# State attention and a hard-swish FFN on one core: another order of the first 700 operations, shorter work in the first softmax, and a last tile copied in two halves

## The chip, the cores and the metric

The kernel runs on one core of a Trainium2 chip. The time is that of the device in microseconds (us), the median of the runs shown; less is better. TensorE is called PE (PEld: its weight loads), VectorE DVE, ScalarE ACT, GpSimd POOL and SyncE SP. SP issues most of the DMAs; ACT can issue them too, from its own queue.

## The reference

For 8 batches (B), 8 heads (H), 512 tokens (S), 32 states (Ns) and 64 columns (D):

```python
scores = scale * np.matmul(x, state.transpose(0, 1, 3, 2))
scores = scores - scores.max(-1, keepdims=True)
a = np.exp(scores)
a /= a.sum(-1, keepdims=True) + 1e-09
xread = np.matmul(a, state)
...
sread = np.matmul(a2, x)
```

`a2` is the same softmax the other way round, of the states over the tokens. The rows of `xread` and `sread` of one batch (512 + 32, heads side by side: 512 columns) go through `h = x @ w_in` (512 x 2048), `g = h * clip(h + 3, 0, 6) / 6` and `g @ w_out` (2048 x 512). All is in 32-bit floats.

## The kernel before, in words

**Tiling.** The work is cut into segments: one for each batch's 512 tokens, and a last one for all 256 state rows. A segment has 16 steps, one for each 128 rows of the hidden layer. A step's first product (`first`, line 959) gives 128 x 512 of h in one of two PSUM banks `ps_h`; ACT adds 3 and takes Relu (L1004), DVE does the minimum and the product (L1006), and g is split into a high and a low part (L306 on ACT, L307 on DVE), so that 32-bit accuracy comes from three matmuls of rounded parts each (L954). The second product (`second`, line 1013) adds g times 128 rows of w_out into four banks `acc0` to `acc3`, one for each 128 tokens (`j`). The weight that the first product uses isn't w_in but w' = state x w_in (`wprime`, line 547, matmuls at L512), so that xread is never made: h = a @ w'.

**The start.** Batch 0 has a way of its own. x and the state are loaded (L481, L438), PE turns them (L622, L593), ACT copies x to `xT` (L626). The turned state is copied four times into `apart` (part of the tile `sread_t`, L607), in two pairs, for either half `u` of the bank's partitions into either half `i` of the target's, and once whole as `stT` (L599): five reads of one bank. `tokens_by_rows` (line 669) makes the first softmax in four parts `q`: scores on PE (L687), maximum, subtraction (L699, L701), exponential on ACT (L704), sum, added constant, reciprocal and product on DVE (L706 to L711). PE turns the result back (L719) and ACT and DVE copy it to `a_first` (L721, L722). The first step (`plain`) takes its products in full 32-bit matmuls (L983, L1023). Weights arrive as 16-bit digits and are put together by ACT (L382) and DVE (L387, called a join here), then split into high and low halves (L414, L416). The big loads of w_in and w_out use tiles that later work needs: a load waits for its place.

**The order.** `Plan` (line 68) holds every operation with an engine (T: PE, V: DVE, S: ACT, Q: SP), a cost, a rank and what it depends on. `order` (line 102) sets them in a row: the first 700 or so are dictated by the list `OPENING`, numbers in the order in which the program adds operations; after it the planner takes the ready one with the lowest rank. Each engine then works through its own operations strictly in that order, so that one that waits holds up all behind it on its engine. `issue` (line 191) also puts matmuls on a constant tile (`wake`, L252; matmuls L1241) into the planned pauses of PE up to the first step. Waits themselves are put in by the framework, from what each instruction reads and writes; it also keeps two engines from using the same PSUM bank at once.

**The end.** The last segment has two tiles `j`. After the last step's second product DVE copies tile 0 out of its bank times 1/6 (L1050) and SP stores it; ACT copies tile 1 (L1047) and stores it from its own queue (L1070, shown with L1065).

Of the kernel before, what the change touches and what calls it, by code (L numbers as in the profile page):

```python
# [10 lines left out]
F32 = mybir.dt.float32  # L11
# [4 lines left out]
BF16 = mybir.dt.bfloat16  # L16
# [51 lines left out]
class Plan:  # L68
# [122 lines left out]
    def issue(self, tc, idle, until):  # L191

        with tc.manual_schedule(
            engines={ENGINE.PE, ENGINE.DVE, ENGINE.Activation, ENGINE.SP}
        ):
            last = 1.0
            for n in self.order():
                if self.ops[n][0] == "T":
                    if self.start[n] <= self.start[until]:
                        gap = self.start[n] - last  # L200
                        for _ in range(int((gap + 0.3) / 0.22) if last < self.WARM else int((gap - 0.25) / 0.13)):
                            idle()
                    last = self.start[n] + self.took[n]
                self.ops[n][3]()
# [3 lines left out]
def tile_state_attention_then_hardswish_ffn(  # L208
# [42 lines left out]
    wake = cpool.tile([P, 256], BF16, name="wake")  # L251
    nc.vector.memset(wake, 1.0)  # L252
# [179 lines left out]
    def load_state(b, rank, after=()):  # L432
        key = ("st_raw", b)

        def load():
            raw = get(key, lambda: att.tile([P, NG, D], F32, name="st_raw", bufs=1))
            for u in range(NG):
                nc.sync.dma_start(raw[:, u, :], st_v[b, :, :, u, :])  # L438
# [9 lines left out]
        if b < TURNED:  # L448
            plan.add("Q", 1.39, rank, load, (), [key], after, 400.0)
            return  # L450
# [137 lines left out]
    def take_in(b, rank, after=(), banks=None):  # L588
# [13 lines left out]
        for u in range(NG) if b < TURNED else ():  # L602
            for i in range(2):
                def put(u=u, i=i):
                    src = bank(st)[u * D : (u + 1) * D, :P].rearrange("p (q n) -> p q n", n=NS)
                    copy = nc.vector.tensor_copy if u == i else nc.scalar.copy
                    copy(apart[i * D : (i + 1) * D, :, u, i], src)  # L607
                (V if u == i else S_)(0.22, RANKS["apart"] if b == 0 else URGENT, put, [st], [("apart", b, u, i)])
# [60 lines left out]
    def tokens_by_rows(after, banks):  # L669
# [6 lines left out]
        whole = lambda: get(bt_key, lambda: outp.tile([P, J, DO], F32, name="ot")).rearrange(  # L676
            "p j e -> p (j e)")[:, : A * NQ * NS]
        wide = lambda t: t.unsqueeze(2).to_broadcast([P, A, NS])
        for q in range(NQ):
# [3 lines left out]
            def scores(q=q, ps=ps):  # L683
# [8 lines left out]
            bt = lambda q=q: whole().rearrange("p (a q n) -> p a q n", q=NQ, n=NS)[:, :, q]  # L692
            m1 = lambda m1_key=m1_key: get(
                m1_key, lambda: small.tile([P, S // NS], F32, name="m1"))[:, :A]
            total = lambda q=q: sums(0).rearrange("p g a -> p (g a)")[:, q * A : (q + 1) * A]
# [5 lines left out]
            shifted = V(0.35, r[1], lambda m1=m1, view=view, bt=bt: nc.vector.tensor_tensor(  # L701
                bt(), view(), wide(m1()), op=ALU.subtract), [m1_key, ps], [part_key])
            first_exps.append(shifted)
            S_(0.38, r[2], lambda bt=bt: nc.scalar.activation(bt(), bt(), AF.Exp, scale=SCALE),  # L704
               [], [part_key])
            V(0.34, r[3], lambda bt=bt, total=total: nc.vector.tensor_reduce(  # L706
                total(), bt(), axis=AX.X, op=ALU.add), [part_key], [sum_key])
            V(0.07, r[3], lambda total=total: nc.vector.tensor_scalar_add(total(), total(), 1e-9),
              [], [sum_key])
            V(0.11, r[3], lambda total=total: nc.vector.reciprocal(total(), total()), [], [sum_key])  # L710
            V(0.35, r[4], lambda bt=bt, total=total: nc.vector.tensor_tensor(  # L711
                bt(), bt(), wide(total()), op=ALU.mult), [sum_key], [part_key])
        for g in range(NG):
            back = (banks[g], ("B", 0, g))

            def turn(back=back, g=g):
                for j in range(J):
                    cols = slice((j * NG + g) * P, (j * NG + g + 1) * P)
                    nc.tensor.transpose(bank(back)[:, j * P : (j + 1) * P], whole()[:, cols], ident)  # L719
            T(0.47, RANKS["turn0"][0], turn, [(*bt_key, q) for q in range(NQ)], [back], after)  # L720
# [4 lines left out]
    def a_first(g):  # L725
        return w_in_of(2, "a", (P, NG, S))[:, g]
# [232 lines left out]
    def first(n):  # L959
        b, i, _, _ = steps[n]  # L960
        ps = ("ps_h", n)
        if b < B:
# [6 lines left out]
            reads += [(*wp_key(b, k), f0, u, h) for u in wide for h in ("hi", "lo")]  # L969
            if plain(b, i):  # L970
                reads = [("w_in2", "a", g) for g in wide]
                reads += [(*PLAIN_WP, f0, u) for u in wide]
# [7 lines left out]
        def run():  # L980
            if plain(b, i):
                for g in wide:
# [7 lines left out]
                [((wh[:, g, fs], wl[:, g, fs]), (ah[:, g, :], al[:, g, :])) for g in wide],  # L990
            )
        first_of[n] = T(1.95 if plain(b, i) else 1.37 if b < B else 1.45, n, run, reads, [ps], first_after.get(n, ()))
# [20 lines left out]
    def second(n):  # L1013
# [3 lines left out]
        for j in range(nt):  # L1017
# [13 lines left out]
            else:  # L1031
                T(0.685, n + LAG + 0.5, run,
# [6 lines left out]
        for j in range(nt):  # L1039
# [6 lines left out]
            elif (j % 2 == 0 or i < NF - 1) if b < B else j == nt - 1:  # L1046
# [13 lines left out]
        else:  # L1060

            ov = out.rearrange("(b s) e -> s b e", s=TOK)
            for j in range(nt):
                rows = slice(S + j * P // B, S + (j + 1) * P // B)
                store = lambda queue, j=j, rows=rows: queue.dma_start(ov[rows], ot()[:, j, :])  # L1065
                if j < nt - 1:
                    Q(n, 262.0, lambda store=store: store(nc.sync), [(*ot_key, j)])
                else:

                    S_(0.6, n, lambda store=store: store(nc.scalar), [(*ot_key, j)])  # L1070
# [146 lines left out]
    for n in range(len(steps)):  # L1217
# [7 lines left out]
        elif b < 1 and n % FPC == 0:  # L1225
            ends = wp_parts[b, c][1:] + [FPC]
            for f0, f1 in zip(wp_parts[b, c], ends):
# [3 lines left out]
                       ["acc2", "acc3"] if n == 0 and f1 < 3 else None,  # L1231
# [9 lines left out]
    plan.issue(tc, lambda: nc.tensor.matmul(awake[:, :256], wake[:, :P], wake, start=True, stop=True), first_of[0])  # L1241
# [30 lines left out]
```

## Time and profile before

| | |
|---|---|
| runs | 648.59, 648.62, 648.96 us |
| median | 648.62 us |
| the profiled execution | 649.16 us |
| its span, first to last instruction | 647.3 us |
| mean granted clock of TensorE | 0.998 |
| PE busy | 639.0 us (99%) |
| DVE busy | 393.3 us (61%) |
| ACT busy | 292.4 us (45%) |

The span is what the profile shows of the program; the profiled execution took 1.9 us more than it. A busy PE isn't PE at its peak, since matmuls are pipelined and overlap in the records. In rows in order of time the columns are: start in us, duration in us, engine, line, operation, out<-in, how many, and in brackets the engine's idle time before it with what ended it. In a table by stage, each engine has its busy time and its number of instructions.

### The profile page before, as it was taken

Reading aid. Unit: us, or ns where it says so; the run is one execution under the profiler, and the core shown is the slowest. Engines: PE = TensorE matmul, PEld = TensorE weight load, DVE = VectorE, ACT = ScalarE, POOL = GpSimd, SP = SyncE. Lnnn points to the kernel's source line nnn. Section 1 sums busy time; section 2 is a strip of 40 time slices with the busy share of each in tenths; the row PEclk is TensorE's granted clock in tenths of the full one; section 3 lists DMA queues with packets and bytes.
Section 4 is the critical chain, followed back from the end, with each engine's and each line's share of the span. In section 5 each row is a group of like instructions: output and inputs, shape, how many; then the busy total and the mean of one; then the engine's idle time right before and its main releaser. Section 6 shows DMA issues by size and latency. Waiting matters only on the chain.

```text
span 647.3 us, 9869 instructions
## 1 busy us (share of the span) xinstructions
PE 639.0 (99%) x3926; PEld 500.9 (77%) x3926; DVE 393.3 (61%) x685; ACT 292.4 (45%) x510; POOL 1.2 (0%) x7
## 2 busy tenths in 40 slices
PE   8999999999999999999999999999999999999997
PEld 6577778787778787787778787787778787888996
DVE  6987985577586366834595366834694444443552
ACT  5986754334343344534344344433353343433442
POOL 0000000000000000000000000000000000000000
PEclk9999999999999999999999999999999999999999
DMA  8996203616531405041231405050222001000101
GB/s 290 381 258 185 70 2 73 96 31 141 127 66 23 75 1 136 3 76 21 70 66 31 68 2 135 8 86 5 82 51 32 1 25 43 0 1 1 65 1 33
DMA packets 135270, 46.25 MB, mean 71 GB/s; under 512 B 123576, under 2 KB 129208, under 8 KB 135096
## 3 DMA queue, kind: packets, MB, share of 16 engines
q1 hardware_dynamic: 135080, 45.36, 28.8%
q8 instruction: 31, 0.51, 0.3%
q10 hardware_dynamic: 144, 0.26, 0.1%
q14 instruction: 15, 0.12, 0.1%
HBM read 33.02 MB, written 8.91 MB: 65 GB/s over the span
## 4 chain that ended last, share of the span: by engine, by line
PE 92%; DVE 3%; DMA 2%; ACT 1%; SPq 1%; issue 0%
PE acc L954 55%; PE ps_h L954 28%; PE ps_s L512 4%; PE ps_h L512 2%; DMA wide<-in_moe_w_in_dram 1%; PE ps_h L911 1%; SPq L499 1%; PE acc L1023 1%; DVE w_in L387 1%; PE ps_h L1241 1%; DVE g L1006 1%; DMA raw<-in_x_dram 0%; DVE m L699 0%; ACT tops L382 0%; DVE g_lo L307 0%
## 5 line engine op out<-in xcount | busy, mean ns | idle before, releaser
L954 PE MATMUL acc<-w_out_hi,g_hi 128*128 128x512 f32 x540 | 213.3, 395 | 0.0
L954 PE MATMUL acc<-w_out_lo,g_hi 128*128 128x512 f32 x540 | 210.5, 390 | 0.0
L954 PE MATMUL acc<-w_out_hi,g_lo 128*128 128x512 f32 x540 | 210.1, 389 | 0.0
L1004 ACT ACTIVATE g<-ps_h,three 128x512 f32<-128x512 f32 (+1 forms) x144 | 95.4, 664 | 217.0 <-PE ps_h L954 217.0
L1006 DVE SCALAR_TENSOR_TENSOR g<-g,ps_h 128x512 f32<-128x512 f32 (+1 forms) x144 | 94.5, 657 | 152.9 <-ACT g L1004 152.0
L954 PEld LDWEIGHTS acc<-w_out_hi,g_hi 128*128 128x128 f32 x540 | 101.4, 188 | 34.2 <-issue 13.8
L307 DVE TENSOR_TENSOR g_lo<-g,g_hi 128x512 fp32r<-128x512 f32 (+1 forms) x143 | 94.2, 659 | 54.0 <-ACT g_hi L306 52.4
L306 ACT CAST g_hi<-g 128x512 fp32r<-128x512 f32 (+1 forms) x143 | 85.3, 596 | 86.7 <-DVE g L1006 77.2
L954 PEld LDWEIGHTS acc<-w_out_hi,g_lo 128*128 128x128 f32 x540 | 101.4, 188 | 21.5
L954 PEld LDWEIGHTS acc<-w_out_lo,g_hi 128*128 128x128 f32 x540 | 101.5, 188 | 19.6
L954 PE MATMUL ps_h<-aT_hi,wp_hi 128*128 128x512 f32 (+1 forms) x246 | 89.9, 365 | 0.4 <-DVE g L1006 0.4
L954 PE MATMUL ps_h<-aT_hi,wp_lo 128*128 128x512 f32 (+1 forms) x246 | 89.0, 362 | 0.0
L954 PE MATMUL ps_h<-aT_lo,wp_hi 128*128 128x512 f32 (+1 forms) x246 | 89.0, 362 | 0.0
L954 PEld LDWEIGHTS ps_h<-aT_hi,wp_hi 128*128 128x128 f32 x246 | 46.4, 189 | 9.6 <-DVE g L1006 1.3
L954 PEld LDWEIGHTS ps_h<-aT_lo,wp_hi 128*128 128x128 f32 x246 | 46.4, 189 | 7.8 <-DVE aT_lo L307 0.2
L954 PEld LDWEIGHTS ps_h<-aT_hi,wp_lo 128*128 128x128 f32 x246 | 46.4, 189 | 7.2
L954 PE MATMUL ps_h<-aT_hi,wp 128*128 128x512 f32 x144 | 50.0, 389 | 0.0
L954 PEld LDWEIGHTS ps_h<-aT_hi,wp 128*128 128x128 f32 x144 | 27.0, 188 | 5.6
L954 PE MATMUL ps_h<-aT_lo,wp 128*128 128x512 f32 x72 | 28.0, 389 | 0.0
L512 PE MATMUL ps_s<-w_in,stT 64*32 64x512 f32 (+1 forms) x320 | 19.6, 548 | 0.0
L612 DVE STREAM_TRANSPOSE tmp<-raw 128x512 f32<-128x512 f32 x28 | 18.6, 692 | 0.3 <-DMA raw<-in_x_dram 0.3
L307 DVE TENSOR_TENSOR wp_lo<-ps_h,wp_hi 128x512 fp32r<-128x512 f32 x18 | 11.8, 687 | 11.0 <-ACT wp_hi L306 10.9
(129 smaller groups left out, 436.3 us busy)
## 6 DMA issues: line engine op xcount, KB each, us to landing
xb<-in_x_dram SPq DMA_DIRECT2D x32, 256.0 KB, 3.9
out_dram<-ot SPq DMA_DIRECT2D x8, 1024.0 KB, 4.3
raw<-in_x_dram SPq DMA_DIRECT2D x112, 64.0 KB, 2.2
early<-in_moe_w_in_dram SPq DMA_DIRECT2D x5, 1023.0 KB, 8.0
raw<-raw SPq DMA_DIRECT2D x112, 32.0 KB, 2.0
raw<-in_moe_w_out_dram SPq DMA_DIRECT2D x7, 511.8 KB, 3.6
wide<-in_moe_w_out_dram SPq DMA_DIRECT2D x2, 1023.5 KB, 10.2
early<-in_moe_w_out_dram SPq DMA_DIRECT2D x2, 1023.5 KB, 5.7
```

The source lines that it names most:

```text
L306: S_(cost, rank, lambda: nc.scalar.copy(hi(), src()), reads, [writes[0]])
L307: V(cost, rank, lambda: nc.vector.tensor_tensor(lo(), src(), hi().bitcast(F32), op=ALU.subtract), [*reads, writes[0]], [writes[1]])
L387: nc.vector.scalar_tensor_tensor(d, low, 13, top_of(i).bitcast(U32), op0=ALU.logical_shift_right, op1=ALU.bitwise_or)
L499: nc.sync.dma_start(t[rows, i].rearrange("t (a c) -> t a c", c=NS), x[b, 4 * g + 2 * i + u, :, k * NS : (k + 1) * NS].rearrange("(a t) c - ...
L512: nc.tensor.matmul(out[u][cols, :], made["stT", b][rows, cols], moving(q)[rows], start=True, stop=True,)
L612: V(0.7, rank[0], lambda q=q, key=key: nc.vector.transpose(xT(b, q), made[key][:, q % 2]), [(*key, q % 2, u, k) for u in range(2) for k in ...
L911: nc.tensor.matmul(bank(pr)[cols, u * D : (u + 1) * D], e2T(b, u)[:, j * P + q * NS : j * P + (q + 1) * NS], x_tile(b)[:, NG * q + u, j, : ...
L954: nc.tensor.matmul(ps, l, r, start=start and k == 0, stop=stop and k == n - 1)
L1004: S_(cost + 0.05, rank, lambda: nc.scalar.activation(g(), bank(ps)[:, :width], AF.Relu, bias=three), [ps], [g_key])
L1006: V(cost, rank, lambda: nc.vector.scalar_tensor_tensor(g(), g(), 6.0, bank(ps)[:, :width], op0=ALU.min, op1=ALU.mult), [ps], [g_key])
L1023: nc.tensor.matmul(bank(acc), made["g_hi", n][:, js], plain_out[i][1](), start=opens, stop=closes)
L1241: plan.issue(tc, lambda: nc.tensor.matmul(awake[:, :256], wake[:, :P], wake, start=True, stop=True), first_of[0])
```

## The change

It has four parts.

1. **First data.** The state's two loads are issued by ACT (`nc.scalar.dma_start`), first of all on that engine, instead of by SP. The four copies into `apart` are given out by the target's half instead of crosswise: DVE writes the lower half, ACT the upper. The constant of the idle matmuls is one of the framework's own (filled by POOL), not a tile filled by DVE, and they are counted from 0.6 instead of 1.0.
2. **First softmax.** Every row of 32 exponentials gets a 33rd element of 1e-9, written once by POOL, so that the sum holds the constant and the four additions go. Reciprocal and product are made for two parts `q` at once (two instead of four of each), and the product is written to a tile of its own (`a_by_rows`, in w_in's place) from which PE turns it back.
3. **The opening's order.** The list `OPENING` is another one. First products of steps 0 to 3 are operations of their own for each of the two groups `g`; the third piece of w' of the first quarter goes into `acc2` and `acc3` as the first two do. In the new list the state is turned before x; the parts of x are worked through in the order 0, 1, 3, 2; two joins instead of three stand before the last product of the softmax; the third piece of w' (`wp b0`, rows 256 to 511) stands before the second step's product instead of after the first step's second product; the join of w_out's second piece (the one that L387 makes from `raw` at 20 us) and the first maximum of the states stand behind g of step 0 instead of before it.
4. **The last tiles.** The last step's first product moves ahead; the second product of the last step but one for tile 1 comes after that of the last step for tile 0; tile 1 is copied in two halves, one by ACT and one by DVE, and both tiles are stored by SP.

```diff
-    "st0": -100.6, "x0": [...]
+    "st0": -600.0, "x0": [...]
...
-5 0 1 3 11 2 4 33 24 80 34 27 93 29 31 32 6 30 28 37 19 41 38 12 14 57 42 43 35 44 58 39 36 59 45 60 13 49 40
+1 0 2 11 5 4 3 24 72 27 85 31 30 28 32 33 19 29 34 35 14 41 36 12 6 46 42 43 39 47 44 37 40 48 45 49 13 58 38
...
-            last = 1.0
+            last = 0.6
...
-    wake = cpool.tile([P, 256], BF16, name="wake")
-    nc.vector.memset(wake, 1.0)
+    wake = nc.const_aps.tensor(1.0, [P, 256], BF16)
...
-                nc.sync.dma_start(raw[:, u, :], st_v[b, :, :, u, :])
+                nc.scalar.dma_start(raw[:, u, :], st_v[b, :, :, u, :])
...
-            plan.add("Q", 1.39, rank, load, (), [key], after, 400.0)
+            plan.add("S", 1.8, rank, load, (), [key], after, 400.0)
...
-                    copy = nc.vector.tensor_copy if u == i else nc.scalar.copy
+                    copy = nc.scalar.copy if i else nc.vector.tensor_copy
...
+        whole = get(bt_key, lambda: outp.tile([P, J, DO], F32, name="ot")).rearrange(
+            "p j e -> p (j e)")[:, : A * NQ * (NS + 1)].rearrange("p (a q n) -> p a q n", a=A, q=NQ)
+        nc.gpsimd.memset(whole[..., NS:], 1e-9)
...
+            V(0.35, r[3], lambda q=q, total=total: nc.vector.tensor_reduce(
+                total(q), whole[:, :, q], axis=AX.X, op=ALU.add), [part_key], [sum_key])
+            if q % 2 == 0:
+                continue
+            pair = slice(q - 1, q + 1)
+            V(0.13, r[3], lambda pair=pair, total=total: nc.vector.reciprocal(total(pair), total(pair)),
+              [(*s1_key, q - 1)], [sum_key])
+            V(0.62, r[4], lambda pair=pair, total=total: nc.vector.tensor_tensor(
+                a_by_rows().rearrange("p (a q n) -> p a q n", q=NQ, n=NS)[:, :, pair], whole[:, :, pair, :NS],
+                total(pair).unsqueeze(3).to_broadcast([P, A, NG, NS]), op=ALU.mult),
+                [sum_key, (*bt_key, q - 1), part_key], [("w_in2", "a", "rows", q)])
...
+        if n < 4:
+            for g in wide:
+                at = T(0.975 if plain(b, i) else 0.685, n, lambda g=g: run([g]), by_group[g], [ps])
...
+            first_of[n] = T(1.37 if b < B else 1.45,
+                            n if n < len(steps) - 1 else n - 0.6, run, reads, [ps], first_after.get(n, ()))
...
-                T(0.685, n + LAG + 0.5, run,
+                T(0.685, n + LAG + 0.5 + (1.2 if b == B and i == NF - 2 and j == nt - 1 else 0.0), run,
...
+            elif b == B and j == nt - 1:
+                for add, engine, cs in (
+                    (S_, nc.scalar.mul, slice(0, DO // 2)), (V, nc.vector.tensor_scalar_mul, slice(DO // 2, DO))
+                ):
+                    add(0.42, rank, lambda j=j, acc=acc, engine=engine, cs=cs: engine(
+                        ot()[:, j, cs], bank(acc)[:, cs], 1.0 / 6.0), [acc], [(*ot_key, j, cs.start)])
...
-                       ["acc2", "acc3"] if n == 0 and f1 < 3 else None,
+                       ["acc2", "acc3"] if n == 0 else None,
```

More of the change, by code (lines that the diff above doesn't have):

```diff
@@ L605, in put @@
                     src = bank(st)[u * D : (u + 1) * D, :P].rearrange("p (q n) -> p q n", n=NS)
-                    copy = nc.vector.tensor_copy if u == i else nc.scalar.copy
+                    copy = nc.scalar.copy if i else nc.vector.tensor_copy
                     copy(apart[i * D : (i + 1) * D, :, u, i], src)
-                (V if u == i else S_)(0.22, RANKS["apart"] if b == 0 else URGENT, put, [st], [("apart", b, u, i)])
+                (S_ if i else V)(0.22, RANKS["apart"] if b == 0 else URGENT, put, [st], [("apart", b, u, i)])
         for q in range(NQ):
@@ L675, in tokens_by_rows @@
         bt_key, s1_key, A = ("ot", ("bt", 0)), ("s1", (0, 0)), J * NG
-        whole = lambda: get(bt_key, lambda: outp.tile([P, J, DO], F32, name="ot")).rearrange(
-            "p j e -> p (j e)")[:, : A * NQ * NS]
+        whole = get(bt_key, lambda: outp.tile([P, J, DO], F32, name="ot")).rearrange(
+            "p j e -> p (j e)")[:, : A * NQ * (NS + 1)].rearrange("p (a q n) -> p a q n", a=A, q=NQ)
+        nc.gpsimd.memset(whole[..., NS:], 1e-9)
         wide = lambda t: t.unsqueeze(2).to_broadcast([P, A, NS])
@@ L691, in tokens_by_rows @@
             view = lambda ps=ps: bank(ps)[:, : A * NS].rearrange("p (a n) -> p a n", n=NS)
-            bt = lambda q=q: whole().rearrange("p (a q n) -> p a q n", q=NQ, n=NS)[:, :, q]
+            bt = lambda q=q: whole[:, :, q, :NS]
             m1 = lambda m1_key=m1_key: get(
                 m1_key, lambda: small.tile([P, S // NS], F32, name="m1"))[:, :A]
-            total = lambda q=q: sums(0).rearrange("p g a -> p (g a)")[:, q * A : (q + 1) * A]
             r = RANKS["soft0"]
@@ L700, in tokens_by_rows @@
                 m1(), view(), axis=AX.X, op=ALU.max), [ps], [m1_key])
[L701 to L712, printed above, removed]
+            if q in ():
+                T(0.46, r[1], lambda m1=m1, ps=ps: nc.tensor.matmul(
+                    bank(ps)[:, : A * NS], minus, wide(m1()), start=False, stop=True), [m1_key], [ps])
+                src, reads = view, [ps]
+            else:
+                V(0.35, r[1], lambda m1=m1, view=view, bt=bt: nc.vector.tensor_tensor(
+                    bt(), view(), wide(m1()), op=ALU.subtract), [m1_key, ps], [part_key])
+                src, reads = bt, []
@@ new lines, in tokens_by_rows @@
+            first_exps.append(S_(0.38, r[2], lambda bt=bt, src=src: nc.scalar.activation(
+                bt(), src(), AF.Exp, scale=SCALE), reads, [part_key]))
+            total = lambda qs: sums(0).rearrange("p g (a q) -> p (g a) q", q=NQ)[:, :, qs]
+            V(0.35, r[3], lambda q=q, total=total: nc.vector.tensor_reduce(
[3 more added lines that the diff above has]
+            pair = slice(q - 1, q + 1)
@@ L717, in turn @@
                 for j in range(J):
-                    cols = slice((j * NG + g) * P, (j * NG + g + 1) * P)
-                    nc.tensor.transpose(bank(back)[:, j * P : (j + 1) * P], whole()[:, cols], ident)
-            T(0.47, RANKS["turn0"][0], turn, [(*bt_key, q) for q in range(NQ)], [back], after)
+                    nc.tensor.transpose(bank(back)[:, place(j)], a_by_rows()[:, place(j * NG + g)], ident)
+            T(0.47, RANKS["turn0"][0], turn, [("w_in2", "a", "rows", q) for q in (1, 3)], [back], after)
             copy = (lambda g=g, back=back: nc.scalar.copy(a_first(g), bank(back)),
@@ L725, in a_first, with a_by_rows @@
     def a_first(g):
-        return w_in_of(2, "a", (P, NG, S))[:, g]
+        return w_in_of(2, "a", (P, 2 * NG, S))[:, g]
+    def a_by_rows():
+        return w_in_of(2, "a", (P, 2 * NG, S))[:, NG:].rearrange("p g s -> p (g s)")
     def halves_of_first(rank):
@@ L969, in first @@
             reads += [(*wp_key(b, k), f0, u, h) for u in wide for h in ("hi", "lo")]
+            by_group = {g: [k for k in reads if k[2 if k[0] == "aT" else -2] == g] for g in wide}
             if plain(b, i):
-                reads = [("w_in2", "a", g) for g in wide]
-                reads += [(*PLAIN_WP, f0, u) for u in wide]
+                by_group = {g: [("w_in2", "a", g), (*PLAIN_WP, f0, g)] for g in wide}
+                reads = [k for g in wide for k in by_group[g]]
         else:
@@ L978, in first, with run @@
             reads += [("wp", (b, k), h) for h in ("hi", "lo")]
-        def run():
+        def run(groups=wide):
             if plain(b, i):
-                for g in wide:
+                for g in groups:
                     nc.tensor.matmul(bank(ps), plain_wp()[:, g, fs],
@@ L989, in run @@
                 bank(ps)[:, :width],
-                [((wh[:, g, fs], wl[:, g, fs]), (ah[:, g, :], al[:, g, :])) for g in wide],
-            )
-        first_of[n] = T(1.95 if plain(b, i) else 1.37 if b < B else 1.45, n, run, reads, [ps], first_after.get(n, ()))
+                [((wh[:, g, fs], wl[:, g, fs]), (ah[:, g, :], al[:, g, :])) for g in groups],
+                groups[0] == wide[0], groups[-1] == wide[-1],
+            )
+        if n < 4:
+            for g in wide:
+                at = T(0.975 if plain(b, i) else 0.685, n, lambda g=g: run([g]), by_group[g], [ps])
+                if n == g == 0:
+                    first_of["begun"] = at
+            first_of[n] = at
+        else:
+            first_of[n] = T(1.37 if b < B else 1.45,
+                            n if n < len(steps) - 1 else n - 0.6, run, reads, [ps], first_after.get(n, ()))
         in_32 = plain(b, i)
@@ L1045, in second @@
                     [acc], [(*ot_key, j)])
-            elif (j % 2 == 0 or i < NF - 1) if b < B else j == nt - 1:
+            elif b == B and j == nt - 1:
[4 more added lines that the diff above has]
+                        ot()[:, j, cs], bank(acc)[:, cs], 1.0 / 6.0), [acc], [(*ot_key, j, cs.start)])
+            elif b < B and (j % 2 == 0 or i < NF - 1):
                 S_(0.62, rank, lambda j=j, acc=acc: nc.scalar.mul(ot()[:, j, :], bank(acc), 1.0 / 6.0),
@@ L1064, in second @@
                 rows = slice(S + j * P // B, S + (j + 1) * P // B)
[L1065 to L1070, printed above, removed]
+                parts = [(*ot_key, j)] if j < nt - 1 else [(*ot_key, j, k * DO // 2) for k in range(2)]
+                Q(n, 262.0, lambda j=j, rows=rows: nc.sync.dma_start(ov[rows], ot()[:, j, :]), parts)
     def w_in_split(c, rank, after):
@@ L1240, in tile_state_attention_then_hardswish_ffn @@
     awake = ps_h.tile([P, 512], F32, name="ps_h")
-    plan.issue(tc, lambda: nc.tensor.matmul(awake[:, :256], wake[:, :P], wake, start=True, stop=True), first_of[0])
+    plan.issue(tc, lambda: nc.tensor.matmul(awake[:, :256], wake[:, :P], wake, start=True, stop=True), first_of["begun"])
 _INS = ["x", "state", "moe_w_in", "moe_w_out"]
```

49 rows, old and new, of tables (OPENING, RANKS) are left out of this document.

## The prediction

> **What bounds the kernel now.** I read the busy time by stage first, then what TensorE (PE) waited for from 22 us on, then the first 27 us and the last 5 us in order of time.
>
> ```profile
> core 0: us, PE busy (x) PEld busy (x) DVE busy (x) ACT busy (x) POOL busy (x), PEclk, DMA share, GB/s
> 0.00:22.00 22.00, 19.09 (x166) 14.17 (x166) 15.53 (x43) 14.94 (x30) 1.17 (x7) 1.00 0.88 312
> 22.00:34.00 12.00, 11.78 (x81) 6.61 (x82) 11.27 (x24) 10.90 (x26) 0.00 (x0) 1.00 1.03 383
> 34.00:62.00 28.00, 27.73 (x151) 21.49 (x149) 22.90 (x38) 21.35 (x36) 0.00 (x0) 1.00 0.89 234
> 62.00:643.00 581.00, 580.41 (x3529) 458.66 (x3529) 343.62 (x583) 245.06 (x420) 0.00 (x0) 1.00 0.23 48
> ```
>
> ```profile
> PE acc L1023 <- DVE g L1006: 0.7, 1, 0.7
> PE ps_h L954 <- DVE g L1006: 0.4, 1, 0.4
> ```
>
> From 62 us on PE is busy 580.41 of 581.00 us at the full granted clock, and after 22 us it waits twice, 0.7 and 0.4 us. So the time is a start, then some 620 us in which PE always has work, then a tail after its last matmul. The change leaves the matmul work of the middle as it is; it can only move the point from which PE is never short of work, add or remove holes before 62 us, and change the tail. In the start VectorE (DVE) carries the path:
>
> ```profile
> 0.74 0.45 SPq L481 DMA_DIRECT2D xb<-in_x_dram  x1
> ...
> 1.19 3.59 PE L1241 MATMUL ps_h<-wake 128*128 128x256 bf16 x16 [1.19 <-DVE three L256]
> 1.25 1.38 SPq L438 DMA_DIRECT2D st_raw<-in_state_dram  x2
> ...
> 4.36 0.87 PEld L622 LDWEIGHTS acc<-ident,xb 128*128 128x128 f32 x4
> ...
> 5.22 0.23 PEld L593 LDWEIGHTS ps_s<-ident,st_raw 128*128 128x128 f32 x1
> ...
> 5.67 0.59 ACT L626 COPY w_in<-acc 128x512 f32<-128x512 f32 x1 [3.44 <-PE acc L622]
> 5.96 0.28 DVE L607 COPY sread_t<-ps_s 64x128 f32<-64x128 f32 x1 [3.75 <-PE ps_s L593]
> ...
> 6.28 0.26 ACT L607 COPY sread_t<-ps_s 64x128 f32<-64x128 f32 x1
> ...
> 6.58 0.29 DVE L607 COPY sread_t<-ps_s 64x128 f32<-64x128 f32 x1 [0.33 <-ACT sread_t L607]
> 6.91 0.26 ACT L607 COPY sread_t<-ps_s 64x128 f32<-64x128 f32 x1 [0.36 <-DVE sread_t L607]
> ...
> 7.20 0.29 DVE L599 COPY stT<-ps_s 128x128 f32<-128x128 f32 x1 [0.32 <-ACT sread_t L607]
> ...
> 7.21 1.10 PE L687 MATMUL ps_s<-sread_t,w_in 128*128 128x64 f32 x8
> ...
> 8.36 0.42 DVE L699 TENSOR_REDUCE m<-ps_s 128x8 f32<-128x256 f32 x1 [0.87 <-PE ps_s L687]
> ...
> 10.05 0.41 DVE L706 TENSOR_REDUCE s<-ot 128x8 f32<-128x256 f32 x1
> ...
> 10.38 0.68 DVE L387 SCALAR_TENSOR_TENSOR raw<-raw,tops 128x512 uint32<-128x512 uint32 x1
> ...
> 10.98 0.17 DVE L708 TENSOR_SCALAR s<-s 128x8 f32<-128x8 f32 x1
> ...
> 15.95 0.75 DVE L711 TENSOR_TENSOR ot<-ot,s 128x256 f32<-128x256 f32 x2
> ...
> 16.75 1.09 PE L719 MATMUL acc<-ident,ot 128*128 128x128 f32 x8 [0.22 <-DVE ot L711]
> ```
>
> The first maximum starts at 8.36 and the last of the four multiplications ends at 16.70: 8.34 us in which DVE hardly pauses, and only then can PE turn the weights back (16.75).
>
> **First data (part 1).** The state's two issues leave SP for ScalarE's (ACT's) queue, ahead of ACT's table load; what ACT's two issues take (1.38 us on SP) lies in its idle time before 5.67 and costs nothing. On SP everything behind them (the other parts of x, the first weights) is issued 1.38 us sooner. The state itself is issued at about 0.74 instead of 1.25. The new order turns the state before x, so the 0.87 us from 4.36 to 5.22 no longer lie ahead of it; and the idle matmuls, now fed by a constant that POOL fills, can start some 0.4 us sooner, with 17 instead of 16 by the count in line 201 (+0.2). By PE's queue the state's turn would come at 4.2, 1.0 us sooner. The trace gives no landing for it: it was there by 5.22, 3.97 us after the issue, so from 0.74 at the latest by 4.71, 0.5 us sooner. I take 0.85, nearer PE's queue, since the wait before 5.22 was on PE's queue and not on the data.
>
> **The state's copies (part 1).** In the rows each copy out of the bank starts 0.03 to 0.04 us after the one before it on the other engine, the stT copy too, which writes nothing the others touch: a chain with a step of about 0.31 us. Four steps stand ahead of the scores now. The new order is DVE, ACT, stT on DVE, ACT, DVE: if every pair keeps waiting, five steps, and ACT's copy of x (0.59) comes behind its second step instead of before its first. From 5.11 (5.96 less 0.85), ACT ends its second copy at 6.3, the copy of x at 6.9, and the scores start at 6.9 instead of 7.21: 0.3 us sooner. The Trainium skill says ("PSUM — Partial Sum Buffer", section "PSUM bank collisions raise a hardware error") that two engines may use one bank together as long as they are in different quadrants of partitions, and must be kept apart otherwise, reads included. The first and last pairs of the new order read different halves of the partitions and write different ones; by that rule they would run side by side, which takes 0.3 us more off. The rows can't decide it: the two halves that waited for each other at 6.91 also write the same partitions. I take 0.3, and 0.6 as the other end.
>
> **The first softmax on DVE (part 2).** From the starts in the rows, a 256-wide operation holds DVE 0.33 us (10.05 to 10.38), a join 0.60 (10.38 to 10.98), two multiplications 0.75 together. Before: 16 x 0.33 (maxima, subtractions, sums, multiplications), 3 x 0.60 for joins, 4 additions and 4 reciprocals at some 0.1 each: 7.9, with 0.4 of pauses. After: 12 x 0.33, two joins ahead of the last multiplication instead of three, two paired multiplications at 0.66 to 0.75, two reciprocals at 0.15: 6.9. The sums run over 33 instead of 32 elements, 3%, in the noise of the row; reading at a step of 33 isn't in the trace, and I bound it by the rows at -0.0 and +0.2. With the pauses kept, 1.1 to 1.2 us less. So the last multiplication ends at 16.70 - 0.3 - 1.2 = 15.2, and the turn back starts 1.5 us sooner.
>
> **From the turn back to the second product (part 3).**
>
> ```profile
> 18.22 1.88 PE L983 MATMUL ps_h<-w_in,tmp 128*128 128x512 f32 x4
> ...
> 21.49 0.68 DVE L1006 SCALAR_TENSOR_TENSOR g<-g,ps_h 128x512 f32<-128x512 f32 x1
> ...
> 22.22 3.87 PE L1023 MATMUL acc<-raw,g 128*128 128x512 f32 x8 [0.73 <-DVE g L1006]
> ...
> 26.02 0.66 PE L512 MATMUL ps_s<-w_in,stT 64*32 64x256 f32 x16
> ```
>
> DVE takes 5.5 us from 16.70 to the end of g at 22.2. The new order gives it three joins there too, and leaves out a maximum of the states (0.60): 4.9 us, so g would be ready at 20.1. PE: first product 1.5 us sooner (from 16.7 on, 1.7 of its 1.88 before the next can start, in two halves, the first without waiting for the second group), then the next piece of w' (0.6), which now goes into acc2 and acc3, then the second step's product, six matmuls like these of the chain of waits (1.59 with their run-out, 1.4 without):
>
> ```profile
> 30.22 1.59 PE ps_h L954 x6
> ```
>
> That makes 20.4 to 20.6. The later counts: the second product starts at 20.5 instead of 22.22, 1.7 us sooner (2.1 by DVE alone). And the piece of w' at 26.02, 0.6 us of PE's time behind the wait of 0.7, is now done in front, in time that PE would spend waiting: another 0.6. Lead 2.3 us.
>
> **What the stages to 62 us give back (part 3).** Between 22 and 34 us DVE is busy 11.27 of 12 and ACT 10.90. DVE now reaches this stage owing a join and a maximum, 1.2 us, that it had done before 22.2; it has 0.73 idle to take them from. So 0.5 us of the lead is lost; nothing at best, 1.6 (with ACT's 1.10 idle used up too) at worst. From 34 to 62 DVE has 5.1 us and ACT 6.6 idle, enough to keep up.
>
> ```profile
> 60.05 0.78 ACT L382 CAST tops<-wide 128x512 f16<-128x512 bf16 x1 [1.96 <-DMA wide<-in_moe_w_in_dram]
> ```
>
> The wait of 0.4 at 62 us has its cause here: ACT stands 1.96 us before a load of w_in, with the product's Relu behind it. The new order issues this load sooner, but PE uses it some 2 us of work sooner as well. Between 0.4 won and nothing, I take 0.2.
>
> **The tail (part 4).**
>
> ```profile
> 638.55 0.48 ACT L1004 ACTIVATE g<-ps_h,three 128x256 f32<-128x256 f32 x1 [1.45 <-PE ps_h L954]
> ...
> 642.60 0.60 ACT L1047 ACTIVATE ot<-acc 128x512 f32<-128x512 f32 x1 [2.67 <-PE acc L954]
> 642.64 0.61 SPq L1065 DMA_DIRECT2D out_dram<-ot  x1
> 643.23 0.66 ACTq L1065 DMA_DIRECT2D out_dram<-ot  x1
> ```
>
> The last tile's own matmuls still end the kernel's PE work; the tile before it ends 0.7 us (three matmuls) sooner, so its copy and store are out of the way. The last copy, 0.60 us on ACT, becomes two halves on DVE and ACT, some 0.42 (10.05's width) and 0.45 (the 0.48 at 638.55 also adds a bias), and both read one bank in all partitions. By the chain of copies above they wait for each other: 0.42 + 0.03 + 0.45 = 0.90 instead of 0.60, 0.3 us later; side by side, 0.15 sooner. The store goes to SP, issue 0.61 instead of 0.66, and its two halves must both be done. I take 0.15 later: the rows speak for waiting, less what the shorter issue and a free queue give back. The same section of the Trainium skill speaks against this edit: by it two engines reading one bank in the same quadrants must be separated, so the split costs 0.3.
>
> **Sum.** -1.7 (start) - 0.6 (piece of w') + 0.5 (given back) - 0.2 (load) + 0.15 (tail) = -1.85, say -1.9 us. The profiled execution took 649.16 us (span 647.3, so 1.9 outside it), 0.5 above the median of 648.62; the same 1.9 from both gives 647.3 profiled and a median of 646.7. A measurement of this kernel can tell 0.2%, 1.3 us, from no change: faster is under 647.3, slower over 649.9.
>
> **Rivals.** (a) The lead is eaten: DVE and ACT can't follow between 22 and 48 us, since the rows leave them 0.73 and 1.10 us of slack in the first of these stages. With 1.6 lost instead of 0.5 and the state at its late bound (0.35), -1.9 becomes -0.5, 648.1: no change. For it: 94% busy; against it: the new order puts early products of the first steps there, which ask little of DVE. 0.19. (b) All good ends at once: halves side by side in the start (-0.3) and the tail (-0.3), nothing given back (-0.5): -3.0, 645.6. By the skill's rule only the first of these would come: -2.2, 646.4, within my own case. 0.08. (c) Slower, by one load.
>
> ```profile
> 15.78 3.80 SPq L373 DMA_DIRECT2D early<-in_moe_w_in_dram  x3
> DMA to landing us min/median/max: 3.6/7.5/10.4
> ```
>
> (The second line is the landing of all such loads up to 40 us.) The new order puts ACT's high halves of the fifth and sixth pieces of w_in ahead of the first w_out halves and of g's high half of step 1; now they come behind them. That load waits for its place until two joins are done, so it is issued at about 15.7 as now, and ACT reaches it at about 22. At a flight of 6.3 us it decides: beyond that ACT stands, and soon PE, one for one. At the median 7.5 it costs 1.2; at 10.4, 4.1: -1.9 + 4.1 = +2.2, 650.8. Against it: the queue ahead of it is issued 1.4 us sooner and drains sooner. 0.06.
>
> **How the numbers follow.** My case 0.67 with its bounds: start 0.35 to the late side and 0.7 to the early, given back 0 to 1.2. The rivals 0.19, 0.08, 0.06. Faster = 0.67 + 0.08 - 0.01 = 0.74; same 0.20, slower 0.06. The range takes in (a) and nearly all of (b): 645.5 to 648.2.
>
> **What would show it.** Right: the state's first copy at about 5.1; last multiplication of the first softmax ending near 15.2 with DVE full from some 8.0; L1023's product at about 20.5; no L512 piece between it and the next steps; PE's waits after it under 1 us together; the end of the last matmul 1.9 to 2.1 us sooner; the two halves of the last copy one behind the other. Wrong: PE waits of over 1 us between 22 and 62 us (then (a), or (c) if ACT stands before an "early" load), or a first maximum no sooner than 8.3.

## The result and the profile after

The changed kernel takes 653.08 us (median of 6 runs, 651.43 to 655.27), the kernel before 648.62 (6 runs, 648.28 to 649.06): 1.0068 times as long, interval 1.0047 to 1.0089. The forecast was 646.7. So it is slower, and by more than the 0.2% that can be told.

The profiled execution took 653.92 us. Its span, and then the table by stage (each engine's busy time in us, instructions in brackets, granted clock, DMA share, GB/s):

```profile
core 0: 652.1 us, clock 0.999
```

```profile
0.00:22.00 22.00, 16.93 (x132) 13.70 (x133) 9.82 (x24) 9.24 (x19) 1.27 (x8) 1.00 0.69 242
22.00:34.00 12.00, 12.00 (x74) 7.13 (x71) 11.77 (x24) 11.43 (x27) 0.00 (x0) 1.00 0.91 332
34.00:62.00 28.00, 28.00 (x178) 20.82 (x177) 24.20 (x43) 22.73 (x41) 0.00 (x0) 1.00 0.98 259
62.00:648.00 586.00, 584.18 (x3546) 461.45 (x3544) 347.82 (x588) 248.85 (x425) 0.00 (x0) 1.00 0.23 50
```

From 22 us on PE is as full as before. The loss is in the first row: DVE did 9.82 us of work there instead of 15.53. The same stretch in order of time (start, duration, engine, line, operation, tiles, count, idle time before it and what ended it):

```profile
0.74 1.76 ACTq L438 DMA_DIRECT2D st_raw<-in_state_dram  x2
...
0.77 3.79 PE L1268 MATMUL ps_h<-const-bfloat16-1.0 128*128 128x256 bf16 x17 [0.77 <-PEq L1283]
...
8.17 0.45 PE L593 MATMUL ps_s<-ident,st_raw 128*128 128x128 f32 x1 [3.61 <-DMA st_raw<-in_state_dram]
...
8.66 0.29 DVE L607 COPY sread_t<-ps_s 64x128 f32<-64x128 f32 x1 [6.69 <-PE ps_s L593]
...
8.98 0.26 ACT L607 COPY sread_t<-ps_s 64x128 f32<-64x128 f32 x1 [4.96 <-DVE sread_t L607]
...
9.27 0.29 DVE L599 COPY stT<-ps_s 128x128 f32<-128x128 f32 x1 [0.32 <-ACT sread_t L607]
9.60 0.26 ACT L607 COPY sread_t<-ps_s 64x128 f32<-64x128 f32 x1 [0.36 <-DVE stT L599]
9.89 0.28 DVE L607 COPY sread_t<-ps_s 64x128 f32<-64x128 f32 x1 [0.33 <-ACT sread_t L607]
...
10.79 3.67 PE L689 MATMUL ps_s<-sread_t,w_in 128*128 128x64 f32 x16
...
12.79 0.42 DVE L700 TENSOR_REDUCE m<-ps_s 128x8 f32<-128x256 f32 x1 [2.62 <-PE ps_s L689]
...
21.70 1.07 PE L730 MATMUL acc<-ident,w_in 128*128 128x128 f32 x8 [0.35 <-DVE w_in L721]
...
27.08 1.51 PE L1047 MATMUL acc<-raw,g 128*128 128x512 f32 x3
```

ACT issues the state first of all, half a us sooner than SP did, and yet PE waits 3.61 us for it and turns it at 8.17 instead of 5.43. Then PE itself is slow: 16 matmuls of the scores take 3.67 us, against 1.10 for 8 before. The second product starts 4.86 us late (27.08 against 22.22), and the last matmul ends 4.81 late (647.37 against 642.56): the whole loss is made before 27 us, and next to nothing of it is made up. The state's turn and the last matmul before:

```profile
5.43 0.42 PE L593 MATMUL ps_s<-ident,st_raw 128*128 128x128 f32 x1
...
642.17 0.39 PE L954 MATMUL acc<-w_out_hi,g_lo 128*128 128x512 f32 x1
```

The tail, from 646.7 us on:

```profile
646.77 2.09 SPq L1097 DMA_DIRECT2D out_dram<-ot  x2
...
646.98 0.39 PE L968 MATMUL acc<-w_out_hi,g_lo 128*128 128x512 f32 x1
...
647.41 0.42 DVE L1075 TENSOR_SCALAR ot<-acc 128x256 f32<-128x256 f32 x1 [0.67 <-PE acc L968]
647.87 0.38 ACT L1075 ACTIVATE ot<-acc 128x256 f32<-128x256 f32 x1 [4.36 <-DVE ot L1075]
```

The halves of the last tile do stand one behind the other. But from the end of the last matmul to the end of the span it is 4.7 us, as before.

### The profile page after: what moved, and what is told of

The parts are those of the page before. It is cut to its first block, busy times and chain, and to the rows that moved or that the text cites. A ratio compares the mean times of both kernels' runs of the same rounds, so it can differ in the third digit from the quotient of the medians.

```text
span 652.1 us, 9876 instructions
## 1 busy us (share of the span) xinstructions
PE 641.1 (98%) x3923; PEld 503.1 (77%) x3923; DVE 393.6 (60%) x677; ACT 292.5 (45%) x510; POOL 1.3 (0%) x8
## 4 chain that ended last, share of the span: by engine, by line
PE 94%; DMA 3%; DVE 1%; issue 0%; ACT 0%; ACTq 0%; DVEq 0%
PE acc L968 56%; PE ps_h L968 29%; PE ps_s L512 4%; PE ps_h L512 2%; DMA wide<-in_moe_w_in_dram 1%; PE ps_h L925 1%; DMA st_raw<-in_state_dram 1%; DMA raw<-in_moe_w_out_dram 1%; PE acc L1047 1%; PE ps_s L689 1%; PE acc L622 1%; PE ps_h L998 0%; ACT tops L382 0%; DVE w_in L721 0%; DVE w_in L387 0%
## 5 line engine op out<-in xcount | busy, mean ns | idle before, releaser
L306 ACT CAST wp_hi<-ps_h 128x512 fp32r<-128x512 f32 x18 | 9.9, 590 | 18.4 <-PE ps_h L512 18.4
```

The costliest lines, as they stand in the source:

```text
L306: S_(cost, rank, lambda: nc.scalar.copy(hi(), src()), reads, [writes[0]])
```

## The experiments

**Theory A:** the state, on ACT's queue, is issued early but lands late, because its 256-byte packets share the DMA engines with the large packets that SP issues at the same time. **A':** PE's pause until then makes the next matmuls slow and costs as much again. **Rival B:** the loss is the new order's (four copies given out by halves, state turned before x, fewer DVE operations); the queue is innocent. Where nothing else is said the base is the changed kernel. The kernel before, on the same chips, had a median of 648.56 us beside the first four experiments, 648.71 beside the one without idle matmuls and 648.53 beside the others.

**Only the queue undone.** The state is issued by SP again, ahead of x:

```diff
-                nc.scalar.dma_start(raw[:, u, :], st_v[b, :, :, u, :])
+                nc.sync.dma_start(raw[:, u, :], st_v[b, :, :, u, :])
```

> The changed kernel with one thing undone: the state's two loads are issued by SP again, first of all on it; all else as changed. Theory A (the state came late because its small packets on ScalarE's queue shared the DMA engines with SP's large ones): the state is turned at 4.2 to 4.7 us, the first maximum starts at 7.7 to 8.2, the turn back at 15 to 15.6, and the time is 646.5 to 647.5 us, faster than the kernel before by 1 to 2. Rival B (the new order of the opening is what costs, in DVE's and ScalarE's stages up to 62 us): the start is earlier in the same way, but the time stays at 650 or above.

649.19 us (12 runs, 648.32 to 651.34), ratio to before 1.001 (0.9993 to 1.0027): 3.9 us of the loss are gone. B falls for the larger part, though the time lies in neither of the two ranges expected. The state's turn came at 4.72, but the turn back at 19.20, not by 15.6. What was left is seen in PE's rows:

```profile
10.23 1.78 PE L622 MATMUL acc<-ident,xb 128*128 128x128 f32 x8 [1.30 <-DMA xb<-in_x_dram]
...
12.02 3.52 PE L689 MATMUL acc<-sread_t,w_in 128*128 128x64 f32 x16
```

With the state in front, the last parts of x land later; PE stands 1.30 us, and the next 16 matmuls take 3.52 us instead of some 2.0. Again a wait, and again a slow stretch behind it.

**Only the queue changed.** The kernel before with the reverse of that edit alone; here ACT issues behind its table load, at 1.19 and 2.38.

> The kernel before with one thing changed: the state's two loads are issued by ScalarE, after its table load; all else as before. Theory A: the state is turned at 7.5 us or later instead of 5.2, and the time is 651 to 653. Rival B: the time stays within 0.5 us of 648.6.

656.37 us (6 runs, 653.34 to 657.91), ratio 1.0107 (1.0076 to 1.0138). The queue alone makes the old kernel slow, and by more than the whole change did (and than the 651 to 653 expected). PE's turn of the state, and the first stage:

```profile
9.15 0.45 PE L593 MATMUL ps_s<-ident,st_raw 128*128 128x128 f32 x1 [4.25 <-DMA st_raw<-in_state_dram]
```

```profile
0.00:22.00 22.00, 16.56 (x110) 13.63 (x118) 8.58 (x26) 8.37 (x16) 1.17 (x7) 0.67 0.71 242
```

**The pause filled.** 37 instead of 17 idle matmuls ahead of the state's turn, the queue left as changed:

```diff
-                        for _ in range(int((gap + 0.3) / 0.22) if ...
+                        for _ in range(37 if last == 0.6 else int((gap + 0.3) / 0.22) if ...
```

> The changed kernel with 37 idle matmuls instead of 17 ahead of the state's turn, so that PE does not stand still for the 3.6 us in which it waits for the state; nothing else differs. Theory A': of the 4.9 us that the turn back lost, some 2 come from matmuls that run at half their rate after that pause (213 against 117 ns from one to the next at L622, 16 of L689 in 3.67 us). Then the first maximum starts 0.8 us sooner, the turn back 2 us sooner, and the time is 650.5 to 651.5, with less spread between runs than 651.4 to 655.3. Rival: the slower matmuls lie beside DVE's work, and the time stays at 652 to 653.

650.52 us (12 runs, 649.66 to 652.46), ratio 1.0028 (1.0013 to 1.0043): 2.56 us less than the changed kernel. PE no longer waits for the state; it turns it at 7.48, when the idle matmuls end.

```profile
0.77 6.87 PE L1268 MATMUL ps_h<-const-bfloat16-1.0 128*128 128x256 bf16 x37 [0.77 <-PEq L1283]
...
7.48 0.27 PE L593 MATMUL ps_s<-ident,st_raw 128*128 128x128 f32 x1
...
9.66 2.00 PE L689 MATMUL ps_s<-sread_t,w_in 128*128 128x64 f32 x16 [0.70 <-ACT w_in L626]
...
18.44 1.07 PE L730 MATMUL acc<-ident,w_in 128*128 128x128 f32 x8 [0.35 <-DVE w_in L721]
```

The same 16 matmuls in 2.00 us instead of 3.67. The state was somewhat sooner in this execution too: all of its 264 packets had gone by 6.5 us, where in the changed kernel's profile it was 200. So the pace is better measured from the state's turn to the turn back: 13.53 us in the changed kernel (8.17 to 21.70), 10.96 here (7.48 to 18.44). A' holds: these 2.57 us are more than half of the loss.

**The state as SP's second load,** where it was before the change; the opening's list begins `0 1 2` instead of `1 0 2`, and the count of idle matmuls becomes 24.

> As the first of these runs, but SP issues the first part of x ahead of the state instead of behind it. Theory A: within 0.5 us of the first of these runs, since the state lands 0.5 us later and x 1.4 us sooner, and both are needed for the first scores; 646.5 to 647.5. Rival B: 650 or above.

648.03 us (12 runs: eleven from 647.41 to 648.46, one 653.42), ratio 0.9994 (0.9975 to 1.0014).

```profile
4.70 0.27 PE L593 MATMUL ps_s<-ident,st_raw 128*128 128x128 f32 x1
...
6.87 2.00 PE L689 MATMUL ps_s<-sread_t,w_in 128*128 128x64 f32 x16 [0.73 <-ACT w_in L626]
8.02 0.42 DVE L700 TENSOR_REDUCE m<-ps_s 128x8 f32<-128x256 f32 x1 [1.49 <-PE ps_s L689]
...
14.86 0.69 DVE L721 TENSOR_TENSOR w_in<-ot,s 128x512 f32<-128x512 f32 x1
...
15.70 1.06 PE L730 MATMUL acc<-ident,w_in 128*128 128x128 f32 x8 [0.35 <-DVE w_in L721]
...
21.07 1.96 PE L1047 MATMUL acc<-raw,g 128*128 128x512 f32 x4
```

All the rest of the change stands here, and it is no slower than before. That ends B. From the state's turn to the turn back it is 11.00 us, as with the pause filled. It is no gain that can be told either: 0.5 us by the medians where I had hoped for 1.9, and outside the 646.5 to 647.5 expected of this run. The same kernel, run again on another chip, says how firm that is.

> The changed kernel with the state's load on SP as its second issue, once more on this chip, as the base of the next two: 648.0 us (647.4 to 648.5), its turn back at 15.7 us. Nothing here tells theories apart.

648.25 us (11 runs, 647.73 to 649.71), ratio 0.9999 (0.999 to 1.0007). In this profiled execution the 24 idle matmuls lasted until 5.5 us instead of 4.9; the state was turned at 5.58 and the turn back came at 16.55, 0.85 later than in the first.

**The state on ACT's queue, SP's large loads held back.** The kernel as changed, but SP's third load waits for three fills of its tile by POOL and is issued at 4.71 instead of 1.74:

```diff
+            for _ in range(3 if (kind, k) == ("out", 0) else 0):
+                nc.gpsimd.memset(pieces(), 0)
             nc.sync.dma_start(flat[:, :, : flat.shape[2] - 1], src)
```

> The changed kernel with the state still on ScalarE's queue, but SP's third load (output weights, 512 KB) waits behind three GpSimd memsets of its own tile, so that SP's queue carries only the first two loads of x until about 5 us. Theory A (the state's 256 small packets are issued early enough and lose their turn to the large packets of SP's queue): the packets go out in one stretch and the state's turn on PE starts at 4.3 to 5.3 us instead of 8.17. Rival (ScalarE's queue is slow by itself, or its issues come too late): the turn stays between 7.5 and 8.5 us. The total is not of interest: the later loads start about 1.5 to 2 us late, so some 650 to 654 us by either theory.

One run. The DMA view (queue q1 is SP's, q10 ACT's: packets, MB, share of the 16 engines), first of the changed kernel, for 2 to 4, 4 to 5 and 5 to 7.5 us:

```profile
q1 hardware_dynamic: 528, 0.56, 95.9%
q10 hardware_dynamic: 132, 0.03, 7.3%
...
DMA packets 85, 0.27 MB, mean 269 GB/s; under 512 B 5, under 2 KB 24, under 8 KB 85
q1 hardware_dynamic: 85, 0.27, 71.8%
...
q1 hardware_dynamic: 668, 0.80, 94.3%
q10 hardware_dynamic: 132, 0.03, 5.8%
```

and of this experiment, for 2.5 to 5 us, with its turn of the state:

```profile
q1 hardware_dynamic: 419, 0.40, 45.4%
q10 hardware_dynamic: 264, 0.07, 11.6%
```

```profile
5.32 0.45 PE L595 MATMUL ps_s<-ident,st_raw 128*128 128x128 f32 x1 [0.76 <-DMA st_raw<-in_state_dram]
```

In the changed kernel half of the state's 264 packets went before 4 us, none in the next us, and the other half after 5, while SP's queue held 72 to 96% of the engines. With SP's queue at 45% all 264 were through by 5 us, from the same queue and the same issue, and the turn came at 5.32 instead of 8.17. So ACT's queue is not slow by itself: what SP sends at the same time makes the state late. In what way stays open. In the us in which none of the state's packets went, SP's queue held 72% of the engines, not all; 61 of its 85 packets were of 2 KB or more, the size of those of the 512 KB load that SP issued at 1.74, and the state's second half was issued at 1.91, just behind it. Whether the engines take the two queues in turn or in the order of issue, no run here tells. (The line numbers of this kernel are two higher.) The total (652.26 us, one run) has SP's late loads in it and says nothing on this.

**No idle matmuls,** with the state as SP's second load: `range(0 if last == 0.6 else ...)` in the line of the 37 above.

> The changed kernel with the state's load on SP as its second issue, and none of the 24 idle matmuls ahead of the state's turn; all loads, copies and their order as with them. If PE's pause costs by itself (after it matmuls are issued at half the pace, 213 instead of 112 ns, until some 3 to 8 us of work have passed, as in the changed kernel): the first 16 matmuls of the scores take 3.6 us instead of 2.0, the first maximum comes at 9 instead of 8.0, the last multiplication ends 1 to 2.5 us later, 649.2 to 650.6 us in all. Rival (the changed kernel was late only because its state was late): scores again in 2.0 us and 648.0 to 648.3 us in all.

650.50 us (11 runs, 648.75 to 651.55), ratio 1.0019 (1.0003 to 1.0035): 2.25 us more than the second run of the same kernel with them, and 2.47 more than the first.

```profile
5.21 0.44 PE L593 MATMUL ps_s<-ident,st_raw 128*128 128x128 f32 x1 [5.21 <-DMA st_raw<-in_state_dram]
...
7.56 3.68 PE L689 MATMUL ps_s<-sread_t,w_in 128*128 128x64 f32 x16 [0.20 <-ACT w_in L626]
...
13.16 3.51 PE L689 MATMUL acc<-sread_t,w_in 128*128 128x64 f32 x16
```

A' by itself, with no load moved: a PE that comes idle to its data costs some 2 us. The state is turned at 5.21 here, between the 4.70 and 5.58 of the two runs with idle matmuls, so its landing is not the cause. The last multiplication of the softmax ends at 20.09, 3.7 us later than in the second of them and more than the 1 to 2.5 expected; part of it is made up behind.

**A better opening.** Two tries to make the good version faster. First, all four block copies on DVE, `stT` last, x's first part turned ahead of the state (`copy = nc.vector.tensor_copy`, and `33 ... 27 34 31 29 30 32 28` in the list):

> The kernel before it in this call, with all four block copies of the state on VectorE instead of two there and two on ScalarE, the third copy of the turned state last, and the first part of x turned ahead of the state. Theory C (from the first maximum at 8.02 us to the turn back at 15.55 VectorE has no idle time, 7.35 of 7.53 us, so the turn back follows the first maximum one for one; and the start of the scores is held by five copies of one PSUM bank one after another, 0.33 us of hand-over each time the engine changes): scores at 6.2 instead of 6.87 us, first maximum at 7.35, turn back at 15.0 if nothing else is late, about 0.6 us less in all, 647.4. Rival (the second half is held by the loads of the third and fourth parts of x, which land at 8.7 and 9.4 us): first maximum at 7.35 but turn back at 15.4 to 15.7, 647.8 to 648.0. Rival (the hand-overs cost nothing, the data lands late): scores stay at 6.8 to 6.9.

648.43 us (12 runs, 647.49 to 651.85), ratio 1.0004 (0.9993 to 1.0016).

```profile
6.06 0.30 PE L593 MATMUL ps_s<-ident,st_raw 128*128 128x128 f32 x1 [1.14 <-DMA st_raw<-in_state_dram]
...
6.48 1.21 DVE L607 COPY sread_t<-ps_s 64x128 f32<-64x128 f32 x4 [4.51 <-PE ps_s L593]
...
7.51 1.97 PE L689 MATMUL ps_s<-sread_t,w_in 128*128 128x64 f32 x16 [0.24 <-DVE sread_t L607]
```

From the state's turn to the first score it is 1.45 us now (6.06 to 7.51) instead of 2.17 (4.70 to 6.87) and 2.20 in the two runs without this; but in the profiled execution the state landed later, the turn back came at 16.25 instead of the 15.0 hoped for, and the whole is no faster. I also had the reason wrong: four copies on one engine take 0.30 us each, hardly less than the 0.31 of a step between engines. What went is one copy and ACT's copy of x, which no longer stands behind the state's. Second, in addition, the first load of output weights issued behind all of x:

> As the one before it in this call, and the first load of output weights is issued behind all of x instead of behind its second part, its two conversions later with it. If the loads of x hold the second half: turn back at 15.0 against 15.4 to 15.7 without this, 647.3 us in all. If VectorE alone holds it: turn back at 15.0 in both, no difference. If weights now land too late for VectorE's conversions: turn back or the second product later than without this, 648 us or more. By each theory part of the lead may be given back at 57 to 61 us, where PE waits for converted input weights (1.09 us there in the run with the state as second load, 0.58 before).

648.66 us (11 runs, 647.94 to 649.38), ratio 1.0001 (0.9993 to 1.001). From the first maximum to the turn back, in this kernel and in the second run with the state second (length, PE, PEld, DVE):

```profile
7.82:15.98 8.16, 7.42 (x98) 5.67 (x98) 7.69 (x19) 5.45 (x11) 0.00 (x0) 1.00 1.02 367
```

```profile
8.92:16.55 7.63, 6.89 (x93) 5.16 (x93) 7.45 (x19) 5.73 (x13) 0.00 (x0) 1.00 1.04 386
```

The turn back comes at 15.98, not 15.0: DVE starts sooner and then has 0.47 us idle instead of 0.18 and works 0.24 us longer. Neither try gains anything that can be told.

## Why the prediction was wrong

**The step that failed is "First data (part 1)":** "what ACT's two issues take ... lies in its idle time before 5.67 and costs nothing", and the state there "from 0.74 at the latest by 4.71, 0.5 us sooner. I take 0.85". It took the flight of a load that SP issued alone and moved it with the time of issue. The turn came 2.7 us later instead of 0.85 sooner, and the start, -1.7 in the sum, came out at +4.86. The runs show in its place: issued from a second queue, the state's small packets are held up by whatever the first queue sends. Only the first of its two loads was issued sooner, too: the second went out at 1.9 us, against 2.1 from SP, since ACT's first issue took 1.15 us. When SP issued the state, its own order kept x's second part and the weights behind it; on ACT's queue nothing does, and the freed SP issued them 1.4 us sooner into the state's flight. The Trainium skill says as much ("DMA: Bandwidth & Descriptors", section "Issuing engines are not separate DMA queues"): loads started by several engines interleave on the same 16 DMA engines, and only the time of issue is saved. The trace agrees that the queues do not run apart: 95.9% and 94.3% for one, 7.3% and 5.8% for the other; that they simply alternate it does not show, since for one us between none of the state's packets went.

**A cost was missing:** the sum gave every matmul its time from the profile of before, where the idle matmuls reach the first data. Behind a pause of 3.61 us that is wrong: the matmuls were issued at half the pace. By the medians it is 653.08 - 648.03 = 5.05 us from the changed kernel to the one with the state as SP's second load, of which filling the pause returns 2.56; the other 2.49 I put down to the lateness itself. But even without these 5 us the change is worth 0.5, not 1.9.

The other steps can be read where the state lands as before (the two runs with the state as SP's second load, against the kernel before):

- *The state's copies.* Right: from the state's turn to the scores it is 2.17 and 2.20 us in the two runs instead of 1.78; the forecast, 0.85 and 0.3 sooner, makes 2.33. That the scores came 0.34 sooner in the first run, close to the 0.3, is luck: in the second they came 0.57 later, behind its longer idle matmuls. And all five copies stand one behind another, at 8.66, 8.98, 9.27, 9.60 and 9.89 in the changed kernel, though the pairs touch different halves. By the releasers in brackets the program makes each wait for the one before it, so the rule of the Trainium skill that I weighed, by which they could run side by side, is not put to the test here.
- *The first softmax on DVE.* Right in sign, too large: 7.53 us from the first maximum to the last multiplication's end (8.02 to 15.55) instead of 8.34, 0.8 less where I took 1.2, and 7.49 in the second run. My own terms, 7.9 before and 6.9 after, give 1.0, not 1.2. Of the sizes, a paired reciprocal holds DVE 0.17 us (11.10 to 11.27) where the next operation does not need it and 0.29 (14.57 to 14.86) where it does, not 0.15.
- *From the turn back to the second product.* Right: 5.37 us there, 5.38 in the changed kernel, 5.3 forecast.
- *The piece of w', what is given back, the load.* Forecast 0.3 more lead by the end. The lead was 1.15 us at the second product and 1.22 at the last matmul (641.34 against 642.56) in the first run, 0.27 and 0.88 in the second: 0.1 and 0.6 more, on either side of the forecast. (Of the 1.22 the medians keep 0.5; the profiled execution before was itself 0.5 over its median.) At the late load of w_in, where I had looked for 0.2 of gain, there was none: PE's wait there is 0.93 us, and 0.51 in the second run, instead of 0.42, with ACT 2.1 us in front of the load instead of 1.96. In the first run:

```profile
59.26 0.50 PE L968 MATMUL ps_h<-aT_hi,wp_lo 128*128 128x512 f32 x1 [0.93 <-DVE wp_lo L307]
```

```profile
ACT tops L382 <- DMA wide<-in_moe_w_in_dram: 2.1, 1, 2.1
```

- *The tail.* The halves wait for each other, as forecast; the time to the end is unchanged, not 0.15 more.

Of the rivals none had the queue in it. (c), slower by one load, was the right kind with the wrong load: I looked for a load that ends late from 16 us on, and the one that the change itself moved I had priced at its issue. The sign that the prediction set for itself, a first maximum no sooner than 8.3, came: 12.79.

## What to carry to other kernels

A load moved to a second queue is issued sooner, but loses its place: price it by what the first queue will send during its flight, and if it is small and needed first, leave it in the one queue ahead of the large ones. Which place there is a matter of what it pushes back: as SP's second load the state cost nothing, as its first it made PE wait 1.30 us for the last parts of x (649.19 against 648.03). When something makes PE wait at the start, count the wait twice: look at how long the same matmuls take behind it. Both can be had from one profile, and idle matmuls that reach to the late data returned the second part here.

## What the runs showed of the hardware

The half pace lasts longer than the pause. Matmuls issued in each us, PE alone (length, busy time and number, granted clock, DMA share, GB/s), in the run with 37 idle matmuls:

```profile
5.00:6.00 1.00, 1.00 (x6) 1.00 0.77 245
6.00:7.00 1.00, 1.00 (x10) 1.00 1.07 349
```

The distance of two matmuls falls from 213 to 112 ns at 6.2 us there, 5.4 us after the first matmul. In every run here the first matmuls go at 213 ns; what differs is when that ends:

- with the state as SP's second load at 3.4 us, 2.7 after the first matmul, and in the second run of that kernel at 4.9, 4.1 after it;
- in the changed kernel, which had not left the half pace before its pause, at 16.2, 8.0 after the end of the pause, with PE busy throughout;
- without idle matmuls at 18.7, 13.5 after the first matmul;
- in the kernel before with the state on ACT's queue, which had left the half pace at 4.0 and fell back into it behind its pause of 4.25 us, at 24.4, 15 after the end of the pause.

Shorter waits can do it too: behind the 1.30 us with the state first on SP the half pace was back at 10.9, but not behind the waits of 1.02 us (second run of the state second) and 1.14 us (copies on DVE). The Trainium skill ("TensorE: Matmul & The Clock Gate", section "Part 1: The HAM clock gate") has the half clock end after a busy window of about 3.4 us; the factor of about two agrees with the trace, the length does not: 2.7 to 15 us here. Nor does the granted clock tell it. A stretch of half pace in the changed kernel, and then one in the kernel before with the state on ACT's queue (PE first, the granted clock third from the end):

```profile
12.00:16.00 4.00, 4.00 (x21) 3.91 (x21) 2.32 (x6) 1.31 (x4) 0.00 (x0) 1.00 1.05 407
```

```profile
16.00:20.00 4.00, 4.00 (x20) 3.62 (x18) 2.37 (x10) 3.21 (x7) 0.00 (x0) 0.50 0.32 129
```

The same pace, 21 and 20 matmuls in 4 us, reads 1.00 in one and 0.50 in the other: it has to be read from the matmuls. And one load, the state's, issued at the same 1.24 us by the same queue behind and ahead of the same loads, was waited for until 6.06 in one execution and was there by 4.70 in another.
